# The seam of two layers: values' weights in other tiles, and the last dense products and the first values' products in one written order

## The chip, the core and the metric

The kernel runs on one core of a Trainium2 chip. The metric is the device time of one execution in microseconds. Before the change it was 1354.75 us, the median of three runs (1354.53 to 1355.81). The kernel's engines are TensorE (products, in the profile PE), VectorE (DVE), ScalarE (ACT) and GpSimd (POOL); its fetches and stores are issued by the SP engine's queue.

## The reference

The input is one sequence of 2048 rows with 640 columns. Two kinds of layer alternate, twice each, all with the same weights:

```python
x = x + _A_ref(_layernorm(x), A_wqkv, A_w_phi, A_wo)   # linear attention
x = x + _B_ref(_layernorm(x), B_w1, B_b1, B_w2)        # dense, Mish, dense
x = x + _A_ref(_layernorm(x), A_wqkv, A_w_phi, A_wo)
x = x + _B_ref(_layernorm(x), B_w1, B_b1, B_w2)
```

The attention has 32 heads of 20 columns. Queries and keys go through a small matrix per head (`w_phi`), and their features are two softmaxes, of the result and of its negative, side by side. The features of the keys times the values are summed over all rows; each query then takes the product of its features with this sum, divided by that with the sum of the features. A product with `wo` follows. The dense part is `h = x @ w1 + b1` with 1536 columns, `h * tanh(softplus(h))`, and a product with `w2`. All of it is float32.

## The kernel before

**Precision.** Each float32 operand is held as a high and a low part, and a product is made of three passes of TensorE: high by high, high by low, low by high. "Splitting" writes the two parts: ScalarE copies the high one (`split`, line 143), VectorE or GpSimd subtracts it for the low one (line 144).

**Blocks.** The 2048 rows are eight blocks (`NB`) of 256; a block is two halves of 128 rows. A layer (`LAYERS` = 2) has three stages: `attend_first` (keys, values and queries of all blocks, and the sum over the keys), `attend_second` (the queries' average and the product with `wo`) and `dense` (both dense products). `dense` walks over 8 blocks by 6 pairs of hidden column blocks: `hidden` makes 60 products (line 941) and the activation (`mish`, lines 951 to 967), and `contract` two steps later (`SKEW`) makes 24 products with `w2` (line 981) into two wide PSUM tiles per block. After the last pair, `end` adds the result to the rows (line 1026), takes their statistics, stores them (line 1032), normalises them into two row tiles (line 128), transposes these in place (line 386) and spills them in eight DMAs (line 388) as columns for the next layer (`n2_d`).

**The seam.** What is looked at here is the passage from `dense` of the first layer to `attend_first` of the second, about 655 to 715 us into the span. The first block's columns are fetched (`load_turned`, line 396) and split (`Transposed.step`, lines 128 and 332) while the last dense pairs run. `load_v_weights` takes the five blocks of 128 rows of the values' weights (line 138) into raw tiles and splits them into the `r1` tiles, which the first dense weights have left; the split's ScalarE instructions are placed behind the last exponential of `mish`. Raw block k stands in a row tile (k = 0, 1), a v tile (k = 2, 3) or a big tile (k = 4); the order is 0, 1, 4, 2, 3 (`V_ORDER`). The columns' weights for keys and queries come from DRAM, where the first layer left them (`load_k_weights`, line 213, and `load_q_weights`, line 207).

In `attend_first` of the second layer, block 0 is worked off in the order values of half 0, keys of half 0, keys of half 1, values of half 1, queries of half 0, queries of half 1. Values of half i are 30 products, 15 for each half of the columns, into two narrow PSUM tiles (`values`, `project`, `project_half`, line 416); keys and queries are 30 products into one wide PSUM tile. ScalarE copies them out. While block b is worked off, the three column chunks of block b + 1 are fetched, at the first step (`fetch_normed`), and split at the fourth to sixth.

**Tiles.** The tags that matter: row tiles ("xn", 4), x tiles of two halves of 640 columns ("x", 2), v tiles ("v", 2), big tiles ("big", 5); in PSUM, wide tiles ("mm", 2) and narrow ones ("one", 4). The three column chunks of a block take three row tiles; the two normalised halves of `end` take two.

**What sets the order.** A planner orders the instructions of each engine from the traced program, by readiness and by the order of tracing. `manual_schedule` holds the written order on the engines that it names; `contract_last`, at the very end of the kernel, does that for TensorE. `issue_after` places instructions behind another on the same engine. All ScalarE instructions that go through `act` are chained in the order in which they are written; those of `split` and `mish` do not go through it. At the seam of the kernel before, nothing is held on TensorE: the planner mixes the last 24 dense products with the values' products.

The lines that the change touches in `dense` and `attend_first`:

```python
nxt, kv_ws = first
...
pv = project(xts, i, kv_ws, D, [one_tile(), one_tile()], ks=V_ORDER)
...
if pr == n_pr - 1:
    end(b)
```

Of the kernel before, what the change touches and what calls it, by code (L numbers as in the profile page):

```python
# [16 lines left out]
P = 128  # L17
S = 2048
D = 640
# [5 lines left out]
BT = 2  # L25
BLK = BT * P
NB = S // BLK
NT = S // P
G = 11
HC = D // 2  # L30
# [7 lines left out]
SKEW = 2  # L38
V_ORDER = (0, 1, 4, 2, 3)
# [12 lines left out]
def kernel(  # L52
# [13 lines left out]
    nc = tc.nc  # L66
# [11 lines left out]
    def one_tile():  # L78
        return psum.tile([P, 512], F32, tag="one", name="one", bufs=4)
# [4 lines left out]
    def x_tile():  # L84
        return work.tile([P, BT, D], F32, tag="x", name="xt", bufs=2)
# [49 lines left out]
    def staged(src, stage):  # L135

        st = stage()[:, :D]
        nc.sync.dma_start(st, src)
        return st
# [42 lines left out]

    def v_weights(ws, low=nc.vector, ahead=False):

        def fetched(k):
            return staged(wv[k * P:(k + 1) * P, :], (row_tile, row_tile, v_tile, v_tile, big_tile)[k])

        st = {}
        if ahead:
            st = {k: fetched(k) for k in V_ORDER}  # L190
            yield
        for k in V_ORDER:
            split(ws[k][0][:, D:2 * D], ws[k][1][:, D:2 * D], st[k] if ahead else fetched(k), low)
            yield
# [205 lines left out]
    def project(xts, t, ws, col, ps=None, w=HC, ks=range(KD)):  # L400

        if ps is None:
            mm = mm_tile()
            ps = [mm[:, 0], mm[:, 1], mm]
        for c in range(2):
            project_half(ps[c], xts, t, ws, col, c, ks, w=w, final=ks[-1])
        return ps
# [65 lines left out]
    def attend_first(layer, x_src, first):  # L473
# [45 lines left out]
                if b == NB - 1:  # L519
                    yield  # L520

        def values(xts, i, v):
            vv = v.rearrange("p (h d) -> p h d", d=DH + 1)
            if i < BT:
                pv = project(xts, i, kv_ws, D, [one_tile(), one_tile()], ks=V_ORDER)
                for c in range(2):
                    act(vv[:, c * H // 2:(c + 1) * H // 2, :DH],
                        pv[c][:, :HC].rearrange("p (h d) -> p h d", d=DH), AF.Copy)
            else:
                pv = project(xts, i % BT, kv_ws, D)  # L530
                act(vv[:, :, :DH].rearrange("p (c h) d -> p c h d", c=2),
                    both(pv).rearrange("p c (h d) -> p c h d", d=DH), AF.Copy)
            act(vv[:, :, DH], ident[:, :H], AF.Copy, scale=0.0, bias=1.0)
            yield

        if first is None:
            E = mybir.EngineType
            with tc.manual_schedule(engines={E.PE, E.SP, E.Activation, E.DVE, E.Pool}):
                written[0] = True
                ps = one_tile()  # L540
                for _ in range(TURNS):
                    nc.tensor.transpose(ps[:, :P], ident, ident)  # L542
                xt = x_tile()
                rows = [row_tile() for _ in range(BT)]
# [24 lines left out]
                kv_ws = [r1_pair(k) for k in range(KD)]  # L569
# [8 lines left out]
                xts = FirstRows()  # L578
# [16 lines left out]
                turned, last = one_tile(), one_tile()  # L595
# [50 lines left out]
                vs = [v_tile() for _ in range(BT)]  # L646
                xt = fetch(x_src, 1)
# [20 lines left out]
                nxt = Transposed(nxt_rows)  # L668
# [15 lines left out]
                    advance()  # L684
                    pending.append(g)
        else:
            nxt, kv_ws = first
            load_k_weights(kv_ws)
            q_ws = load_q_weights()
        for b in range(0 if layer else 1, NB):  # L690
            xts = nxt
            order = ("k0", "k1", "v0", "v1", "q0", "q1")
            if b == 0:
                order = ("v0", "k0", "k1", "v1", "q0", "q1")
            elif b == 1 and layer == 0:
                order = ("k0", "q0", "k1", "v0", "q1", "v1")
            elif b == NB - 1:
                order = ("k0", "k1", "v0", "v1", "q0")
            vs = [v_tile() for _ in range(BT)]
            for n, (kind, t) in enumerate(order):  # L700
                t = int(t)
                i = b * BT + t
                if b == 0 and n == 1:
                    kva = one_tile()
                    nc.vector.memset(kva[:, :360], 0.0)
                if b == NB - 1 and n == 3:
                    loaded = {0: load(0), 1: load(1, lambda: x_tile().rearrange("p t d -> p (t d)"))}
                if b + 1 < NB:
                    if n == 0 and b == 1 and layer == 0:
                        with tc.issue_after(ready):  # L710
                            xt = fetch_normed(b + 1)
                    elif n == 0:
                        xt = fetch_normed(b + 1)
                    elif n == 2:
                        nxt = xt if layer else normed(b + 1, xt)
                    elif n > 2:
                        nxt.step()
                g = {"k": lambda: keys(xts, i, vs[t]), "q": lambda: queries(xts, i),
                     "v": lambda: values(xts, i, vs[t])}[kind]()
                if b == NB - 1 and n == 3:  # L720
                    advance()
                    next(g)
                else:
                    next(g)
                    advance()
                pending.append(g)
            if 0 < b <= KD and layer == 0:
                spill_qk_weights(kv_ws, q_ws, b - 1)
            if b == 1:
                five = make_five(KD, lambda k: wo[k * P:(k + 1) * P, :], ordered=True)  # L730
                next(five)
                o_ws = []
            elif 2 < b:
                o_ws.append(next(five))
# [192 lines left out]
    def dense(x_src, x_dst, w1s, w2s, first, last):  # L927
# [41 lines left out]
        def contract(b, pr, ah, al):  # L969
            final = last and b == NB - 1  # L970
            if pr == 0:
                blocks[b][2] = [mm_tile() for _ in range(BT)]
                if final:
                    blocks[b].append(one_tile())
            pys = blocks[b][2]

            def product(t, j, c, n):
                f = 2 * pr + j
                l, w = ((ah, 0), (ah, 1), (al, 0))[n]
                ps = blocks[b][3] if final and t == c == 1 else pys[t][:, c]  # L980
                nc.tensor.matmul(ps[:, :HC], l[:, j, t * P:(t + 1) * P], w2s[f][w][:, c * HC:(c + 1) * HC],  # L981
                                 start=(f == 0 and n == 0), stop=(f == KF - 1 and n == 2))

            order = [(t, j, c, n) for t in range(BT) for j in range(2) for c in range(2) for n in range(3)]
            if b == NB - 1 and pr == KF // 2 - 1:
                order = [(t, j, c, n) for j in range(2) for t in range(BT) for c in range(2) for n in range(3)]
            for o in order:
                product(*o)

        def contract_last(b, acts):  # L990
            pys, apart = blocks[b][2:]
# [58 lines left out]
        for i in range(len(steps) + SKEW):  # L1050
            if i < len(steps):
                b, pr = steps[i]
                if pr == 0 and b + 1 < NB:
                    fetch_rows_of(b + 1)
                if pr == 2 and b + 1 < NB:
                    blocks[b + 1] = [fetch(x_src, b + 1), None, None]
                if pr == 3 and (b + 1 < NB or not last):
                    nxt = load_turned(n1_d[b + 1] if b + 1 < NB else n2_d[0], (v_tile, v_tile, row_tile))
                acts[i] = hidden(b, pr)
                if b == 0 and pr == n_pr - 2:  # L1060
                    with tc.issue_after(exps[0]):
                        nxt.step()
                if pr == 1 and b + 1 < NB:
                    with tc.issue_after(exps[0]):
                        normalize(b + 1, ahead, ahead)
                    spill_turned(ahead, n1_d[b + 1])
                if pr == n_pr - 1 and (b + 1 < NB or not last):
                    if b + 1 < NB:
                        blocks[b + 1][1] = nxt
                    with tc.issue_after(exps[0]):  # L1070
                        nxt.all()
            if i <= KD:
                with tc.issue_after(exps[0]):
                    w = next(last_w2)
                if i:
                    w2s[6 + i] = w
            if i == len(steps) - 1 and not last:
                with tc.issue_after(exps[0]):
                    kv_ws = load_v_weights()
            if i >= SKEW:  # L1080
                b, pr = steps[i - SKEW]
                if not last or b < NB - 1 or pr < n_pr - 2:
                    contract(b, pr, *acts.pop(i - SKEW))
                elif pr == n_pr - 1:
                    contract_last(b, {pr - 1: acts.pop(i - SKEW - 1), pr: acts.pop(i - SKEW)})
                if pr == n_pr - 1:
                    end(b)
        return nxt, kv_ws

    with tc.block(schedule_with_timeline_sim=True):  # L1090
        src, first = x, None
# [81 lines left out]
```

## Time and profile before

| | |
|---|---|
| median of three runs | 1354.75 us |
| the profiled execution | 1355.98 us |
| its span, first to last instruction | 1354.1 us |
| TensorE busy | 1348.3 us, 12890 products |
| VectorE busy | 1069.7 us |
| ScalarE busy | 584.6 us |
| GpSimd busy | 468.9 us |
| moved by DMA | 169.21 MB |

The profile is of one execution. A row of an engine's timeline gives the start and the duration in us, the engine, the line of the kernel, the operation, the tiles written and read, their shapes and how many were merged; in brackets, the idle time of the engine before and what released it. A row of the stretches gives, for a window, busy time and number of instructions of TensorE, its weight loads, VectorE, ScalarE and GpSimd, then the granted clock of TensorE (1.00 is full), the busy share of the DMA engines and GB/s. A row of the waits gives who waited for whom: total us, times, longest. Products are pipelined, so the recorded 0.31 us of one is longer than the 0.146 us from one to the next.

### The profile page before, as it was taken

Reading aid. Unit: us, or ns where it says so; the run is one execution under the profiler, and the core shown is the slowest. Engines: PE = TensorE matmul, PEld = TensorE weight load, DVE = VectorE, ACT = ScalarE, POOL = GpSimd, SP = SyncE. Lnnn points to the kernel's source line nnn. Section 1 sums busy time; section 2 is a strip of 40 time slices with the busy share of each in tenths; the row PEclk is TensorE's granted clock in tenths of the full one; section 3 lists DMA queues with packets and bytes.
Section 4 is the critical chain, followed back from the end, with each engine's and each line's share of the span. In section 5 each row is a group of like instructions: output and inputs, shape, how many; then the busy total and the mean of one; then the engine's idle time right before and its main releaser. Section 6 shows DMA issues by size and latency. Waiting matters only on the chain.

```text
span 1354.1 us, 30937 instructions
## 1 busy us (share of the span) xinstructions
PE 1348.3 (100%) x12890; PEld 1336.8 (99%) x12890; DVE 1069.7 (79%) x1810; ACT 584.6 (43%) x1039; POOL 468.9 (35%) x357
## 2 busy tenths in 40 slices
PE   9999999999999999999999999999999999999999
PEld 9999999999999999999999999999999999999998
DVE  7988888886787888778779888888768776676775
ACT  6344444222554555445444344432236444444443
POOL 3345544444322222122225556744441211111112
PEclk9999999999999999999999999999999999999999
DMA  9623336798613543334573534468964231233200
GB/s 345 176 49 73 79 60 132 195 281 275 207 28 88 118 117 85 54 97 114 147 225 69 114 71 77 81 159 241 286 242 121 79 83 27 88 98 98 66 33 21
DMA packets 350757, 169.21 MB, mean 125 GB/s; under 512 B 287241, under 2 KB 324089, under 8 KB 350617
## 3 DMA queue, kind: packets, MB, share of 16 engines
q1 hardware_dynamic: 350617, 167.23, 46.3%
q8 instruction: 101, 1.65, 0.5%
q14 instruction: 39, 0.32, 0.1%
HBM read 104.61 MB, written 62.59 MB: 123 GB/s over the span
## 4 chain that ended last, share of the span: by engine, by line
PE 99%; DMA 1%; issue 0%; ACT 0%; DVE 0%; POOL 0%; SPq 0%; POOLq 0%
PE mm L416 28%; PE one L941 25%; PE mm L981 24%; PE one L416 13%; PE mm L801 3%; PE one L326 2%; PE one L501 2%; PE mm L273 1%; DMA v<-in_wv 1%; PE one L542 0%; PE mm L999 0%; DMA r1l<-wp_d 0%; PE one L273 0%; PE one L981 0%; PE one L801 0%; PE one L999 0%
## 5 line engine op out<-in xcount | busy, mean ns | idle before, releaser
L967 POOL TENSOR_TENSOR ol<-big,ol 128x512 fp32r<-128x512 f32 (+1 forms) x98 | 130.6, 1332 | 484.7 <-ACT ol L966 400.7
L981 PE MATMUL mm<-r2h,ol 128*128 128x320 f32 x1236 | 295.5, 309 | 0.0
L941 PE MATMUL one<-xtl,r1h 128*128 128x256 f32 x960 | 268.2, 279 | 0.0
L941 PE MATMUL one<-xth,r1l 128*128 128x256 f32 x960 | 268.0, 279 | 0.0
L941 PE MATMUL one<-xth,r1h 128*128 128x256 f32 x960 | 265.9, 279 | 0.0
L981 PEld LDWEIGHTS mm<-r2h,ol 128*128 128x128 f32 x1236 | 211.9, 188 | 0.0
L981 PE MATMUL mm<-r2l,ol 128*128 128x320 f32 x618 | 190.6, 309 | 0.0
L416 PE MATMUL mm<-r1h,xth 128*128 128x304 f32 (+1 forms) x600 | 185.1, 309 | 0.0
L416 PE MATMUL mm<-r1h,xtl 128*128 128x304 f32 (+1 forms) x600 | 183.8, 307 | 0.0
L416 PE MATMUL mm<-r1l,xth 128*128 128x304 f32 (+1 forms) x600 | 183.6, 306 | 0.0
L941 PEld LDWEIGHTS one<-xtl,r1h 128*128 128x128 f32 x960 | 180.4, 188 | 0.0
L941 PEld LDWEIGHTS one<-xth,r1l 128*128 128x128 f32 x960 | 180.4, 188 | 0.0
L941 PEld LDWEIGHTS one<-xth,r1h 128*128 128x128 f32 x960 | 179.6, 188 | 0.0
L956 DVE TENSOR_SCALAR big<-big 128x512 f32<-128x512 f32 (+1 forms) x98 | 56.3, 575 | 111.4 <-ACT big L954 111.2
L465 POOL TENSOR_TENSOR big<-big,r 128x1280 f32<-128x1280 f32 x42 | 101.4, 2419 | 69.3 <-DVE r L464 44.4
L954 ACT ACTIVATE big<-one,b1s 128x256 f32<-128x256 f32 x192 | 80.8, 467 | 91.1 <-PE one L941 90.2
L958 ACT ACTIVATE big<-big,two 128x512 f32<-128x512 f32 (+1 forms) x98 | 70.1, 716 | 115.4 <-DVE big L957 115.4
L966 ACT ACTIVATE ol<-big 128x512 fp32r<-128x512 f32 (+1 forms) x98 | 60.9, 622 | 133.5 <-DVE big L965 133.4
L981 PEld LDWEIGHTS mm<-r2l,ol 128*128 128x128 f32 x618 | 116.1, 188 | 0.0
L416 PEld LDWEIGHTS mm<-r1h,xth 128*128 128x128 f32 x600 | 112.8, 188 | 0.6
L416 PEld LDWEIGHTS mm<-r1h,xtl 128*128 128x128 f32 x600 | 112.8, 188 | 0.4
L416 PEld LDWEIGHTS mm<-r1l,xth 128*128 128x128 f32 x600 | 112.8, 188 | 0.0
(186 smaller groups left out, 3147.3 us busy)
## 6 DMA issues: line engine op xcount, KB each, us to landing
big<-e_d SPq DMA_DIRECT2D x30, 640.0 KB, 6.5
x_d<-xt SPq DMA_DIRECT2D x23, 640.0 KB, 5.1
e_d<-r SPq DMA_DIRECT2D x88, 160.0 KB, 4.0
xt<-x_d SPq DMA_DIRECT2D x22, 640.0 KB, 5.6
n_d<-xn SPq DMA_DIRECT2D x176, 80.0 KB, 2.2
xt<-in_x SPq DMA_DIRECT2D x15, 640.0 KB, 4.3
xn<-x_d SPq DMA_DIRECT2D x28, 320.0 KB, 4.2
v<-n_d SPq DMA_DIRECT2D x30, 256.0 KB, 3.4
```

What stands on the lines that cost most here:

```text
L326: nc.tensor.transpose(ps[:, c, t * P:(t + 1) * P], self.rows[t][:, (c0 + c) * P:(c0 + c + 1) * P], ident)
L416: nc.tensor.matmul(ps[:, :w], a[:, sl], r, start=(k == 0 and n == 0), stop=(k == final and n == end))
L465: nc.gpsimd.tensor_tensor(eg, eg, r.unsqueeze(2).to_broadcast([P, 2 * H, DH]), op=ALU.mult)
L501: nc.tensor.matmul(kva[32 * q:32 * q + DH + 1, c:c + 2 * DH], v[:, (DH + 1) * h:(DH + 1) * (h + 1)], e[:, 2 * DH * h:2 * DH * (h + 1)], st ...
L801: nc.tensor.matmul(po[c][64 * q:64 * q + 64, GW * j:GW * j + w], phs[g][:n, s0:s0 + 64], kvb[:n, g, :w], start=True, stop=True)
L941: nc.tensor.matmul(ph[:, j, :], l, r, start=(n == 0), stop=(n == 3 * KD - 1))
L954: exps[0] = nc.scalar.activation(part(ta, 0)[:, j - js.start], ph[:, j, :], AF.Exp, bias=b1s[:, 2 * pr + j:2 * pr + j + 1]).ins
L956: nc.vector.tensor_scalar_min(e, e, E_CAP)
L958: nc.scalar.activation(r, n, AF.Ln, bias=two)
L966: nc.scalar.activation(ah[:, js], n, AF.Copy)
L967: nc.gpsimd.tensor_tensor(al[:, js], n, ah[:, js].bitcast(F32), op=ALU.subtract)
L981: nc.tensor.matmul(ps[:, :HC], l[:, j, t * P:(t + 1) * P], w2s[f][w][:, c * HC:(c + 1) * HC], start=(f == 0 and n == 0), stop=(f == KF - 1 ...
```

## The change

The raw blocks k = 2 and 3 of the values' weights go into the two halves of one x tile, and block 4 into a row tile. (In the first layer, where `ahead` is set, the homes stay as they were.)

`contract` of the last pair of the first layer's last block issues nothing any more. It returns two functions, one for each of its two hidden column blocks, and `dense` returns them together with a third that calls `end` of that block. A new function, `between_layers`, calls them in `attend_first` of the second layer, at the first step of block 0, after the fetch of block 1's chunks has been traced. It holds TensorE's order by `manual_schedule`: 30 values' products of half 0, twelve dense products, six values' products of half 1, twelve dense products, and nine more values' products; `end` is traced ahead of these nine. Among the twelve, the eight that read the activation's high part stand first. The other 15 values' products of half 1 stay where they were, in `values`.

```diff
     def v_weights(ws, low=nc.vector, ahead=False):
 
+        halves_of_x = []
+
+        def x_half():
+            if not halves_of_x:
+                xt = x_tile()
+                halves_of_x.extend(xt[:, t] for t in range(BT))
+            return halves_of_x.pop(0)
+
         def fetched(k):
-            return staged(wv[k * P:(k + 1) * P, :], (row_tile, row_tile, v_tile, v_tile, big_tile)[k])
+            home = v_tile if ahead else x_half
+            return staged(wv[k * P:(k + 1) * P, :], (row_tile, row_tile, home, home, big_tile if ahead else row_tile)[k])
...
-        def values(xts, i, v):
+        def between_layers(xts, closing):
+            ps = [one_tile(), one_tile(), one_tile()]
+
+            def products(i, seq):
+                for n, (c, k, j) in enumerate(seq):
+                    rows, w = ((xts.hs, 0), (xts.hs, 1), (xts.ls, 0))[j]
+                    nc.tensor.matmul(ps[i + c][:, :HC], rows[k][:, i // 2 * P:(i // 2 + 1) * P],
+                                     kv_ws[k][w][:, D + c * HC:D + (c + 1) * HC],
+                                     start=(k == j == 0), stop=((k, j) == last))
+
+            with tc.manual_schedule(engines={mybir.EngineType.PE}):
+                last = 4, 2
+                for c in range(2):
+                    products(0, [(c, k, j) for k in (0, 1) for j in range(3)] + [(c, 4, 0), (c, 4, 1)])
+                products(0, [(c, k, j) for c in range(2) for k in (2, 3) for j in range(2)])
+                products(0, [(c, k, 2) for k in (2, 3, 4) for c in range(2)])
+                closing[0]()
+                last = V_ORDER[-1], 2
+                rest = [(0, k, j) for k in V_ORDER for j in range(3)]
+                products(2, rest[:6])
+                closing[1]()
+                closing[2]()
+                products(2, rest[6:])
+            return ps[:2], ps[2:]
+
+        def values(xts, i, v, pv=None):
             vv = v.rearrange("p (h d) -> p h d", d=DH + 1)
             if i < BT:
-                pv = project(xts, i, kv_ws, D, [one_tile(), one_tile()], ks=V_ORDER)
+                if pv is None:
+                    pv = project(xts, i, kv_ws, D, [one_tile(), one_tile()], ks=V_ORDER)
+                elif len(pv) == 1:
+                    pv.append(one_tile())
+                    project_half(pv[1], xts, i, kv_ws, D, 1, V_ORDER, final=V_ORDER[-1])
...
-            nxt, kv_ws = first
+            nxt, kv_ws, closing = first
...
+                if b == n == 0:
+                    pvs = between_layers(xts, closing)
                 g = {"k": lambda: keys(xts, i, vs[t]), "q": lambda: queries(xts, i),
-                     "v": lambda: values(xts, i, vs[t])}[kind]()
+                     "v": lambda: values(xts, i, vs[t], pvs[t] if b == 0 else None)}[kind]()
...
-            order = [(t, j, c, n) for t in range(BT) for j in range(2) for c in range(2) for n in range(3)]
             if b == NB - 1 and pr == KF // 2 - 1:
-                order = [(t, j, c, n) for j in range(2) for t in range(BT) for c in range(2) for n in range(3)]
-            for o in order:
-                product(*o)
+                return [lambda j=j: [product(t, j, c, n) for ns in ((0, 1), (2,)) for t in range(BT)
+                                     for c in range(2) for n in ns] for j in range(2)]
+            for t in range(BT):
+                for j in range(2):
+                    for c in range(2):
+                        for n in range(3):
+                            product(t, j, c, n)
...
-                    contract(b, pr, *acts.pop(i - SKEW))
+                    closing = contract(b, pr, *acts.pop(i - SKEW))
...
-                if pr == n_pr - 1:
+                if pr == n_pr - 1 and (last or b < NB - 1):
                     end(b)
-        return nxt, kv_ws
+        return None if last else (nxt, kv_ws, closing + [lambda: end(NB - 1)])
```

## The prediction

> **What bounds the kernel.** I read the shares of the engines first, then the same by stretches, then the list of who waited for whom on TensorE, and last, round the seam of the two layers, the chain and each engine in order of time.
>
> ```profile
> span 1354.1 us, 30937 instructions
> PE 1348.3 (100%) x12890; PEld 1336.8 (99%) x12890; DVE 1069.7 (79%) x1810; ACT 584.6 (43%) x1039; POOL 468.9 (35%) x357
> ...
> 680.00:700.00 20.00, 19.62 (x135) 19.35 (x134) 13.73 (x30) 7.44 (x16) 4.46 (x5) 1.00 0.75 255
> 700.00:1020.00 320.00, 319.19 (x3731) 314.04 (x3730) 266.12 (x409) 118.07 (x206) 164.90 (x110) 1.00 0.59 151
> ...
> PE one L542 <- POOL ident masks.py:199: 1.3, 1, 1.3
> PE mm L801 <- issue: 0.8, 1, 0.8
> PE one L416 <- ACT r1h L143: 0.4, 1, 0.4
> ```
>
> TensorE is the bound: 1348.3 of 1354.1 us busy, at a granted clock of 1.00 in the stretches shown (the column after POOL). Only three of its waits are listed, and the change bears on the last, 0.4 us at the seam. The number of products does not change. So the change can win no more than that wait; what it can lose has no such limit, since any lateness of another engine that reaches TensorE adds to the time. Here is that wait:
>
> ```profile
> 684.16 6.93 DMA v<-in_wv
> ...
> 691.11 0.75 ACT r1h L143
> ...
> 682.07 1.36 ACT L143 ACTIVATE r1h<-xn 128x640 fp32r<-128x640 f32 x2
> ...
> 691.75 0.40 ACT L966 ACTIVATE ol<-big 128x256 fp32r<-128x256 f32 x1
> 692.06 0.72 ACT L143 ACTIVATE r1h<-v 128x640 fp32r<-128x640 f32 x1
> ...
> 685.64 0.60 PE L416 MATMUL one<-r1h,xth 128*128 128x320 f32 x3
> ...
> 691.90 0.71 PE L416 MATMUL one<-r1h,xth 128*128 128x320 f32 x3 [0.38 <-ACT r1h L143]
> ...
> 696.41 0.30 PE L416 MATMUL mm<-r1h,xth 128*128 128x304 f32 x1
> ...
> 704.98 2.19 PE one L416 x15
> ```
>
> The last two blocks of the values' weights (k = 2, 3) go into v tiles, whose fetch starts at 684.16 and lands 6.9 us later; ScalarE splits the first at 691.11 and the second at 692.06, and only then can TensorE go on. From 685.64 to 696.41 TensorE works off 69 products: 30 values' products of the first half block, 15 of the second half block's first columns, and the last 24 of the dense block. At 2.19 / 15 = 0.146 us each these need 10.1 us; they took 10.77. The seam therefore costs 0.7 us, the listed 0.38 and the slower restart round it.
>
> **The change part by part.** *Other homes for the weights.* The same five fetches and five splits are made; blocks 2 and 3 go to halves of an x tile, block 4 to a row tile instead of a big one. When can they start?
>
> ```profile
> L1032 SPq DMA_DIRECT2D x_d<-xt x2: 337/359/381, 656.8 to 697.0; - x2
> 671.11 0.43 SPq L138 DMA_DIRECT2D xn<-in_wv  x1
> 681.06 0.39 SPq L138 DMA_DIRECT2D big<-in_wv  x1
> ```
>
> The store of the x tile of block 6 is issued at 656.8, so blocks 2 and 3 can come in more than 20 us before use; block 4 can follow the second row tile at 671.11 instead of starting at 681.06. The bytes on the queues are the same, only their order moves; the columns' weights loaded after them are first needed at 696.41, while the last of all these fetches has landed by 692.06, when its split starts, so I cost their shift at nothing. If that cover were gone, each block that is 1 us late would cost 1 us. This step takes away the 0.7 us: **-0.7**. Bounds: 0 (the fetches stay late) to -0.7.
>
> *The written order.* TensorE now takes k = 0, 1, 4 of both column halves, then k = 2 and 3, then the low x products, then twelve dense products, six values' products, twelve dense products, and nine values' products. Nothing is added; a strict order can wait where the old one went round. The earliest risk is the low part of block 4, the eighth product, wanted at 685.64 + 7 x 0.146 = 686.66.
>
> ```profile
> 685.18 0.81 DVE L144 TENSOR_TENSOR r1l<-xn,r1h 128x640 fp32r<-128x640 f32 x1
> 685.91 0.68 DVE L332 TENSOR_TENSOR xtl<-v,xth 128x512 fp32r<-128x512 f32 x1
> 686.50 0.42 DVE L332 TENSOR_TENSOR xtl<-xn,xth 128x256 fp32r<-128x256 f32 x1
> 686.84 0.42 DVE L963 SCALAR_TENSOR_TENSOR big<-big 128x256 f32<-128x256 f32 x1
> 688.57 0.83 DVE L144 TENSOR_TENSOR r1l<-big,r1h 128x640 fp32r<-128x640 f32 x1 [1.31 <-ACT r1h L143]
> ```
>
> VectorE has no gap from 685.18 to 687.26. If the low part of block 4 follows directly on that of block 1, it ends at 685.91 + 0.83 = 686.74, 0.1 us late; behind the three instructions that now follow, it ends near 687.2 + 0.8 = 688.0, 1.3 us late. I take **+0.1**, because its high part can follow the two that end at 682.07 + 1.36 = 683.43 and be there at 684.2, and block 1's low part went ahead of the others too; the bounds are 0 and +1.3. The dense factor's second half is wanted 48 products on (30 + 12 + 6), at 692.65; it was written from 691.75 to 692.15 even behind the late splits, so it is early enough.
>
> *The end of the last dense block moves.* Before, its adds, statistics, two normalised row tiles and eight spills are traced ahead of layer 1; now they stand behind the fetch of block 1's three column chunks, which take row tiles of the same four. What moves is two adds, six statistics, three small instructions on GpSimd, two scalings, two normalisings, two transposes, a store and eight spills. On the queue of fetches it goes behind three entries of 0.5 us (1.04 for two, below) that can be issued long before it; on VectorE and GpSimd nothing of layer 1 is ready before it.
>
> ```profile
> 697.43 1.04 SPq L396 DMA_DIRECT2D xn<-n_d  x2
> 701.83 0.88 SPq L388 DMA_DIRECT2D n_d<-xn  x2
> ...
> 703.94 2.17 SPq L388 DMA_DIRECT2D n_d<-xn  x4
> ...
> 706.28 2.81 SPq L396 DMA_DIRECT2D xn<-n_d  x2
> ...
> SPq L396 <- DMA n_d<-xn: 1.9, 2, 1.4
> ```
>
> I read from this that the tiles of one tag are given out in the order in which the program first uses them: the row tile of the weights' block 1 was last read at 685.99 (685.18 + 0.81), yet the first two chunks are fetched only at 697.43, beside the normalising; the third comes at 706.28, after a spill has freed a row tile. In the new order the three chunks come first and take three of the four, long before they are used. The first normalised half gets the fourth. The second half gets none until the first has been spilled, since the chunks are read later on the same engine. ScalarE's instructions here are chained in the written order, so everything behind that normalising waits too, and first of all the copy of the first values out of PSUM.
>
> ```profile
> 700.00 1.74 ACT L128 ACTIVATE xn<-xt,stats 128x640 f32<-128x640 f32 x2 [7.21 <-DVE stats L305]
> 701.64 0.73 ACT L128 ACTIVATE v<-one 128x320 f32<-128x320 f32 x2
> 702.39 0.67 ACT L128 ACTIVATE big<-mm 128x608 f32<-128x608 f32 x1
> ...
> L128 ACT ACTIVATE v<-one x4: 415/423/437, 701.6 to 707.2; 128x320 f32<-128x320 f32 x4
> ...
> 700.96 1.66 DVE L386 STREAM_TRANSPOSE xn<-xn 128x640 f32<-128x640 f32 x2 [0.88 <-ACT xn L128]
> ...
> DMA to landing us min/median/max: 2.2/2.3/2.4
> ...
> 704.81 0.31 PE L416 MATMUL one<-r1h,xth 128*128 128x320 f32 x1
> ...
> 695.14 1.56 DVE L1026 TENSOR_TENSOR xt<-mm,xt 128x640 f32<-128x640 f32 x2 [1.16 <-PE mm L981]
> ```
>
> The price: the first half's normalising starts at 700.00, its four spills go out from 701.83 to 703.4 (the second half's follow at 703.94), and with 2.3 us to land (the spills issued from 701 to 703) the tile is free at 705.7. The second half starts then instead of 700.87, so what follows is 4.8 us later, with the signalling 5.0. The values' first copy ended at 701.64 + 0.44 = 702.08. There are four narrow PSUM tiles, and the 15 products at 704.81 need a fifth, the one that this copy empties: a cover of 2.7 us. The dense products now end 0.8 us earlier (the add at 695.14 can start near 694.35), which widens the cover by 0.1 against products that come 0.7 us earlier. So TensorE waits 5.0 - 2.8 = **+2.2** us ahead of those 15 products. It has nothing else to do there: the queries' products need a wide PSUM tile, and both hold keys, which are copied still later. The bounds: 0, if the row tiles are given out otherwise, and about 5.0, if the spills land as slowly as the slowest of the sixteen of this stretch (5.1 instead of 2.3; the row below).
>
> ```profile
> 711.40 0.68 ACT L128 ACTIVATE r<-mm 128x608 f32<-128x608 f32 x1 [1.13 <-PE mm L416]
> ...
> 696.57 8.40 PE mm L416 x60
> ...
> DMA to landing us min/median/max: 2.2/2.6/5.1
> ```
>
> Further on, ScalarE is 5.0 - 0.8 = 4.2 us later than now and the products 1.5: the first queries' copy, which ended at 712.08, falls back by 2.7 us. The 15 products end at 704.98 + 2.19 = 707.17; its wide tile is next taken 60 products on, at 8.40 us for 60, so at 715.57: a cover of 3.5. I cost that at nothing and allow 1 us in the range; without the cover each microsecond would count.
>
> *The sum*: -0.7 + 0.1 + 2.2 = +1.6 us. The profiled execution took 1355.98, 1.9 us of it around the span, and stands 1.2 us over the median of 1354.75; the difference is added to both: 1357.6 for such an execution and **1356.35** for the median.
>
> **The rivals.** *A, the seam's gain is left alone*: no row tile is missing, because the three chunks are fetched only after the normalising. For it: that is how they stand now, at 697.43. Against it: they are now written first. It gives -0.7, or 1354.05.
>
> *B, the splits of block 4 come last on VectorE as well*: +1.3 instead of +0.1, everything behind it shifts along; 1354.75 - 0.7 + 1.3 + 2.2 = 1357.55. Against it: VectorE is idle from 687.26 to 688.57 and again later, so the late weights are what set its order now.
>
> *C, slower*: the first half's spills are held on the queue of fetches. Place: the second normalising. A spill that lands in 5.1 us, or one entry ahead of it that waits for its tile, adds 2.8 or more to 2.2; the wait is then 5 us and the time 1354.75 - 0.7 + 5.0 = 1359.05. It decides once the wait passes 3.4 us (0.7 + 2.7). If the array came back from such a gap at half its speed, the 15 products behind it would take another 2.2 us, which makes 1361.2; the rows show a clock of 1.00 with no wait over 1.3 us, so they cannot tell. [...] For it: the slowest spill of the stretch; against it: its neighbours at 701 to 703 all landed within 2.4, and the chunks that fill the queue then would have been fetched long before.
>
> *D, the weights do not come earlier*: the fetches stay behind the columns' weights, the wait of 0.7 remains and the rest comes on top; 1357.0. Against it: the x tile's store is issued at 656.8, and nothing else of this stretch takes such a tile.
>
> **How the numbers follow.** A measurement of this kernel tells about 0.2% from no change, here 2.7 us. My forecast has 0.48, A 0.24, B and D together 0.12, C 0.14, and 0.02 is for something that I have not seen which makes TensorE's own work shorter. The low end is A less the scatter of the runs, 1353.8; the high end lies between B and C, 1358.6, and leaves about a tenth of C above it. Faster by over 0.2% would need 2.7 us where the seam offers 0.7: 0.02. Slower by over 0.2% is C and the upper edge of B and of the forecast: 0.17. The rest, 0.81, is within.
>
> **What the profile after would show.** The fetches of the weights all issued before 680 (first step); no TensorE wait for ScalarE's split between 685 and 696, and the keys' first product near 695.7 (second); the three chunks of block 1 fetched before 697, a gap of some 5 us between the two normalising instructions on ScalarE, and a TensorE wait of about 2 us for the values' copy, ahead of the 15 products, near 704 (third). The prediction is wrong if the two normalising instructions still stand together, or if a wait shows up on TensorE between 685 and 696 of over 1 us.

## The result and the profile after

The changed kernel took 1357.09 us, the median of 22 runs (1356.11 to 1361.39), beside 1355.80 us for the kernel before in as many runs on the same chips (1354.38 to 1357.17). The medians are 1.3 us apart. The ratio over all runs is 1.0014, with a 95% interval of 1.0008 to 1.0020: 1.9 us slower, 1.1 to 2.7. That is within 0.2%, but on the slow side and clear of the scatter. The kernel before stood 1.05 us higher in these runs than in the three that the prediction was made from (1354.75), so the forecast is held against the differences and not against the time itself.

The list of TensorE's waits in the kernel after: who waited for whom, total us, times, longest.

```profile
PE one L425 <- ACT v L128: 1.8, 1, 1.8
PE one L580 <- POOL ident masks.py:199: 1.3, 1, 1.3
PE one L282 <- DMA raw<-in_wqk_t: 0.5, 1, 0.5
```

The wait for the split of the weights is gone; in its place there is a longer one, 1.8 us instead of 0.4, for the copy of the first values (line 128 on ScalarE). The third row is at the start of the kernel and has nothing to do with the change. ScalarE and VectorE round that wait, in order of time:

```profile
681.67 1.98 ACT L143 ACTIVATE r1h<-xn 128x640 fp32r<-128x640 f32 x3
683.56 1.35 ACT L143 ACTIVATE r1h<-xt 128x640 fp32r<-128x640 f32 x2
...
698.81 0.92 ACT L128 ACTIVATE xn<-xt,stats 128x640 f32<-128x640 f32 x1 [8.36 <-DVE stats L314]
704.41 0.92 ACT L128 ACTIVATE xn<-xt,stats 128x640 f32<-128x640 f32 x1 [4.68 <-DMA n_d<-xn]
705.24 0.74 ACT L128 ACTIVATE v<-one 128x320 f32<-128x320 f32 x2
...
684.36 1.55 DVE L144 TENSOR_TENSOR r1l<-xn,r1h 128x640 fp32r<-128x640 f32 x2
685.83 1.56 DVE L144 TENSOR_TENSOR r1l<-xt,r1h 128x640 fp32r<-128x640 f32 x2
```

All five blocks of weights are split before 687.4. The two normalising instructions, which stood together before, are 5.6 us apart, and the bracket of the second names what it waited for: a spill of the first half. The chunks that took the row tiles are in the queue's order of time:

```profile
673.22 0.66 SPq L138 DMA_DIRECT2D xn<-in_wv  x1
...
684.98 1.99 SPq L405 DMA_DIRECT2D xn<-n_d  x3
...
700.64 7.58 SPq L397 DMA_DIRECT2D n_d<-xn  x8
```

The last raw block is issued at 673.22, the three chunks of block 1 at 684.98, some 14 us ahead of the first normalising. Now TensorE at both ends of the wait, and the granted clock behind it (the column after GpSimd's busy time):

```profile
695.36 0.30 PE L425 MATMUL mm<-r1h,xth 128*128 128x304 f32 x1
...
703.62 0.30 PE L425 MATMUL mm<-r1h,xtl 128*128 128x304 f32 x1
705.70 0.41 PE L425 MATMUL one<-r1h,xth 128*128 128x320 f32 x1 [1.78 <-ACT v L128]
...
705.70:707.00 1.30, 1.30 (x9) 1.30 (x10) 0.66 (x2) 1.30 (x5) 0.00 (x0) 1.00 0.00 0
707.00:708.00 1.00, 1.00 (x6) 1.00 (x6) 1.00 (x2) 1.00 (x4) 0.00 (x0) 0.62 0.79 127
708.00:710.00 2.00, 2.00 (x10) 2.00 (x9) 2.00 (x4) 0.91 (x3) 1.28 (x1) 0.50 0.66 105
710.00:711.00 1.00, 1.00 (x7) 1.00 (x6) 1.00 (x2) 0.00 (x0) 0.00 (x0) 0.68 0.00 0
711.00:713.00 2.00, 2.00 (x16) 2.00 (x15) 1.78 (x3) 0.86 (x1) 0.00 (x0) 1.00 0.50 156
```

The 15 products start 1.94 us after the step that the stream before them would have kept. And then the clock falls: to 0.50, from about 707.2 to 710.6. That is 3.4 us at half speed (0.38 + 1.0 + 0.32 us lost of the clock in the three rows, doubled), in which a product takes 0.27 us instead of 0.146.

**A measure that is free of the scatter.** Two waits, which no part of the change touches, come and go from one execution to the next: the one for the first fetch of raw weights (0 to 1.1 us in the profiles of this study) and one in `attend_second` (listed as "issue") for nothing that the profile shows (0 to 1.3 us). Together they move the time of an execution more than the seam's 0.7 us. So beside the times I use a stretch of TensorE's chain that has neither in it: from the start of the last pair's 30 hidden products, just ahead of the seam, to the fourth sum over keys of the second layer. What happens behind its end it does not hold. In the chain of the kernel before its two ends are

```profile
675.26 3.51 PE one L941 x30
...
802.36 1.41 PE one L501 x126
```

and in that of the kernel after

```profile
674.86 3.50 PE one L981 x30
...
804.60 1.40 PE one L510 x126
```

so 127.10 and 129.74 us: the changed kernel loses 2.64 us there.

### The profile page after: what moved, and what is told of

Read it like the earlier page. It is cut to its first block, busy times and chain, and to the rows that moved or that the text cites. A ratio compares the mean times of both kernels' runs of the same rounds, so it can differ in the third digit from the quotient of the medians.

```text
span 1355.6 us, 30939 instructions
## 1 busy us (share of the span) xinstructions
PE 1348.6 (99%) x12890; PEld 1337.2 (99%) x12890; DVE 1067.7 (79%) x1810; ACT 584.6 (43%) x1039; POOL 470.9 (35%) x357
## 4 chain that ended last, share of the span: by engine, by line
PE 98%; DMA 0%; DVE 0%; SPq 0%; ACT 0%; POOL 0%; issue 0%; POOLq 0%; ACTq 0%
PE mm L425 28%; PE one L981 25%; PE mm L1021 24%; PE one L425 13%; PE mm L841 3%; PE one L335 2%; PE one L510 2%; PE mm L282 1%; PE mm L1042 0%; PE one L537 0%; PE one L282 0%; DMA raw<-in_wqk_t 0%; PE one L1021 0%; PE one L841 0%; DMA n_d<-xn 0%; ACT xn L128 0%
```

## The experiments

The table holds every run: the stretch (end less start in the chain of that run's profile), its difference from the kernel before, TensorE's wait ahead of the 15 products, whether the granted clock falls to 0.50 there, and the ratio of the times to the kernel before with its interval.

| run | stretch | difference | wait | clock falls | ratio |
|---|---|---|---|---|---|
| before | 802.36 - 675.26 = 127.10 | 0 | 0 | no | 1 |
| after | 804.60 - 674.86 = 129.74 | +2.64 | 1.78 | yes | 1.0014 (1.0008 to 1.0020) |
| e1, end before the fetch | 802.08 - 675.60 = 126.48 | -0.62 | 0 | no | 1.0002 (0.9993 to 1.0010) |
| e5, end in big tiles | 801.47 - 674.99 = 126.48 | -0.62 | 0 | no | 0.9996 (0.9987 to 1.0005) |
| e2, homes alone | 802.50 - 674.98 = 127.52 | +0.42 | 0 | no | 1.0003 (0.9994 to 1.0012) |
| e3, end behind the fetch alone | 803.64 - 675.14 = 128.50 | +1.40 | 1.46 | no | 1.0015 (1.0006 to 1.0024) |
| e4, old homes | 810.92 - 675.11 = 135.81 | +8.71 | 1.80 | yes, twice | 1.0072 (1.0059 to 1.0086) |
| e6, wait filled with 18 | 804.26 - 676.10 = 128.16 | +1.06 | 0 | no | 1.0014 (1.0005 to 1.0023) |
| e7, wait filled with 9 | 803.85 - 675.67 = 128.18 | +1.08 | 0.8 | no | 1.0009 (1.0001 to 1.0018) |
| e9, wait filled with 4 | 803.26 - 675.01 = 128.25 | +1.15 | 1.4 | no | 1.0006 (0.9997 to 1.0015) |
| e8, after again | 805.14 - 675.43 = 129.71 | +2.61 | 1.76 | yes | 1.0013 (1.0004 to 1.0023) |
| e10, a longer wait | 807.07 - 675.13 = 131.94 | +4.84 | 3.65 | yes | 1.0040 (1.0026 to 1.0054) |

**e1: the end of the dense block is traced ahead of the fetch.**

```diff
+                if b == n == 0:
+                    pvs = between_layers(xts, closing)
                 if b + 1 < NB:
...
-                if b == n == 0:
-                    pvs = between_layers(xts, closing)
```

> The changed kernel, but the last dense block's end (its adds, normalising and spills, with the whole written order) is traced ahead of the fetch of block 1's three chunks instead of behind it, so the two normalised halves get their row tiles before the chunks do. If the row tiles are the cause (theory): the two normalising instructions stand together again, TensorE does not wait ahead of the 15 values' products (1.78 us in the changed kernel), its clock stays at 1.00 behind them, and only the seam's gain is left: 0.5 to 0.9 us faster than the kernel before, some 2 to 2.5 us faster than the changed one. Rival (the written order itself delays the values' copy): the wait stays near 1.8 us and the time 1 to 2 us over the kernel before.

The two normalising instructions stand together, and TensorE has no wait between 684 and 712 us. ScalarE in order of time, and TensorE's stretches:

```profile
699.54 1.74 ACT L128 ACTIVATE xn<-xt,stats 128x640 f32<-128x640 f32 x2 [8.36 <-DMA raw<-in_wo]
701.18 0.74 ACT L128 ACTIVATE v<-one 128x320 f32<-128x320 f32 x2
...
684.00:703.00 19.00, 19.00 (x134) 19.00 (x133) 12.20 (x26) 7.13 (x16) 4.50 (x5) 1.00 0.70 231
703.00:715.00 12.00, 12.00 (x87) 12.00 (x86) 11.13 (x14) 6.30 (x12) 5.87 (x4) 1.00 0.54 114
```

The stretch is 0.62 us shorter than before. The expected 0.5 to 0.9 us in the times did not show: the medians are level (1355.62 and 1355.66). The times cannot show so little: the ratio's interval reaches from 0.9993 to 1.0010, and this run's profile happened to have both of the unrelated waits:

```profile
PE mm L841 <- issue: 1.3, 1, 1.3
PE one L282 <- DMA raw<-in_wqk_t: 1.0, 1, 1.0
```

So the place of the end behind the fetch was the cause of the new wait; TensorE's written order was not, since it is unchanged here.

**e5: the end's two halves in other tiles.** The order of the changed kernel, but tiles of another tag.

```diff
-                xn = [row_tile() for _ in range(BT)]
+                xn = [big_tile()[:, :D] if b == NB - 1 else row_tile() for _ in range(BT)]
```

> The changed kernel, but the two normalised halves of that one end stand in big tiles instead of row tiles; the order of everything else as in the changed kernel. Theory: with tiles at hand the second normalising follows the first at once and the time is that of the run with the end ahead of the fetch: 0.5 to 0.9 us faster than the kernel before. Rival (it is the order of the traced work and not the tile that holds the second half): the gap of some 4.7 us between the two stays, and the time is that of the changed kernel.

```profile
698.93 1.74 ACT L128 ACTIVATE big<-xt,stats 128x640 f32<-128x640 f32 x2 [8.36 <-DVE stats L314]
700.57 0.74 ACT L128 ACTIVATE v<-one 128x320 f32<-128x320 f32 x2
```

No gap, and the same stretch as e1 to the hundredth. Between two runs that remove the wait in different ways, by order and by tile, this leaves the shortage of row tiles as its cause. At 1355.01 us e5 has the lowest median of the experiments, and its stretch is shorter than that of both kernels; against the kernel before (1355.66 beside it) the times do not separate it (0.9996, 0.9987 to 1.0005).

**e2: the new homes alone**, in the kernel before.

```diff
-            return staged(wv[k * P:(k + 1) * P, :], (row_tile, row_tile, v_tile, v_tile, big_tile)[k])
+            home = v_tile if ahead else x_half
+            return staged(wv[k * P:(k + 1) * P, :], (row_tile, row_tile, home, home, big_tile if ahead else row_tile)[k])
```

> The kernel before with only the first part of the change: the raw blocks 2 and 3 of the values' weights in an x tile and block 4 in a row tile; no written order, the end of the dense block where it was. Theory: the late fetch was the whole cause of the seam's wait, so the homes alone win it: no wait of TensorE for the split between 685 and 696 us, 0.5 to 0.9 us faster than the kernel before. Rival (the written order is needed for the gain): a wait of 0.3 us or more stays at the seam and the time is within 0.3 us of the kernel before.

The theory failed. The split is no longer waited for, but the planner puts the dense products later among the values': the last twelve now stand directly ahead of the keys' first product (694.20 to 696.0), where six values' products stood between in the kernel before. Two other waits come up:

```profile
689.84 0.56 PE L990 MATMUL mm<-r2h,ol 128*128 128x320 f32 x2 [0.21 <-POOL ol L976]
696.45 0.41 PE L425 MATMUL mm<-r1h,xth 128*128 128x304 f32 x1 [0.33 <-DVE xt L1035]
```

0.21 us for the activation's low part, and 0.33 us because the keys' wide tile is not yet emptied by the last adds. Together 0.54 us in place of 0.38. The seam's gain needs both: the weights early and the written order, which puts nine values' products between the dense products and the keys.

**e3: the move alone**, in the kernel before: the end is traced behind the fetch, with old homes and no written order.

```diff
-                if pr == n_pr - 1:
+                if pr == n_pr - 1 and (last or b < NB - 1):
                     end(b)
...
+                if layer and b == n == 0:
+                    closing()
                 g = {"k": lambda: keys(xts, i, vs[t]), "q": lambda: queries(xts, i),
```

> The kernel before with only the move: the end of the first layer's last dense block is traced behind the fetch of block 1's three chunks; old homes, no written order. Theory: the second normalised half waits for the spills of the first, a gap of 4.5 to 5 us on ScalarE, TensorE waits some 1.5 to 2.2 us for the values' copy, and its clock drops to half behind that wait for about 3.4 us, which costs some 1.5 us more: 2.5 to 4 us slower than the kernel before. Rival (the gap on ScalarE is only harmful together with the earlier fetches or the written order): under 1 us slower.

```profile
691.75 0.71 PE L416 MATMUL one<-r1h,xth 128*128 128x320 f32 x3 [0.35 <-ACT r1h L143]
706.27 0.41 PE L416 MATMUL one<-r1h,xth 128*128 128x320 f32 x1 [1.46 <-ACT v L128]
```

The old wait at the seam is still there and the new one comes on top; the stretch is 1.40 us longer. The move alone makes the wait. The drop of the clock, which I had expected, is not in this profile, and so the stretch falls short of the expected 2.5 to 4 us. The median of the times was 2.3 us over that of the kernel before. Part of the difference lies behind the stretch: near the end of the span, at 1348.43, this profile has one more wait that the kernel before has not,

```profile
PE mm L1001 <- POOL ol L969: 0.4, 1, 0.4
```

for the low part of an activation in the last dense block. Only e4 has one like it; why it comes up in these two is open.

**e4: the old homes under the written order.**

```diff
-            home = v_tile if ahead else x_half
-            return staged(wv[k * P:(k + 1) * P, :], (row_tile, row_tile, home, home, big_tile if ahead else row_tile)[k])
+            return staged(wv[k * P:(k + 1) * P, :], (row_tile, row_tile, v_tile, v_tile, big_tile)[k])
```

> The changed kernel with the old homes of the raw weights (blocks 2 and 3 in v tiles, block 4 in a big tile), so the written order meets the late fetches. Theory: the strict order cannot go round them; block 4's low part is ready near 689.4 (fetch at 681, split at 687.8, low part at 688.57) but wanted at 686.7, so TensorE waits 2 to 3 us there, and again 2 to 3 us for blocks 2 and 3: 3 to 6 us slower than the changed kernel. Rival (the order is harmless in itself): no more than 1 us over the changed kernel.

```profile
688.24 0.41 PE L528 MATMUL one<-r1h,xth 128*128 128x320 f32 x1 [1.71 <-ACT r1h L143]
689.10 0.63 PE L528 MATMUL one<-r1l,xth 128*128 128x320 f32 x1 [0.45 <-DVE r1l L144]
692.40 0.43 PE L528 MATMUL one<-r1l,xth 128*128 128x320 f32 x1 [0.23 <-DVE r1l L144]
693.39 0.41 PE L528 MATMUL one<-r1h,xth 128*128 128x320 f32 x1 [0.56 <-ACT r1h L143]
694.25 0.42 PE L528 MATMUL one<-r1l,xth 128*128 128x320 f32 x1 [0.45 <-DVE r1l L144]
712.06 0.41 PE L416 MATMUL one<-r1h,xth 128*128 128x320 f32 x1 [1.80 <-ACT v L128]
```

A strict order stops at the first late operand: five waits of 3.4 us in all at the seam where the planner's order has 0.38, and a drop of the clock behind the first as well as behind the last. Of the two groups of waits, 2.2 us for block 4 are as expected, and 1.2 us for blocks 2 and 3 are less. The stretch is 6.1 us longer than in the changed kernel and the median 7.0 us over that of e8 beside it, just over the expected 3 to 6; the waits are 3.4 us of it and the additional drop of the clock some 1.5; about 1 us of the stretch I have not found.

**e8: the changed kernel once more**, unaltered, beside the runs with the filled wait.

> The changed kernel as it is, beside the two with the filled wait. Theory: some executions keep the clock and some lose it, so its times scatter over 3 us or more, while those with the filled wait keep within about 1 us; the profile shows the wait of 1.8 us and, if the clock fell in that execution, 0.5 between 706 and 712 us. Rival: its scatter is that of the kernel before.

The wait of 1.76 us and the drop of the clock are there again, and the stretch agrees with the first profile to 0.03 us. In these rows the stretches are of TensorE alone (busy time, number, granted clock, DMA's share, GB/s):

```profile
PE one L425 <- ACT v L128: 1.8, 1, 1.8
...
706.00:708.00 2.00, 1.76 (x8) 0.67 0.15 25
708.00:710.00 2.00, 2.00 (x9) 0.50 0.88 142
710.00:712.00 2.00, 2.00 (x16) 0.98 0.02 2
```

The scatter of the times says little: 3.7 us here, 3.2 in the kernel before beside it. But the mean granted clock of every execution is on record, to a thousandth, and one drop takes 1.7 us of 1356, or 0.00125. In e8 four executions have a mean of 1.000 and took 1356.0 to 1357.5 us; six have 0.999 or 0.998 and took 1358.5 to 1359.7. Of the 22 runs of the result, 13 have 1.000 (median 1356.67) and nine have less (median 1358.89). So some 15 of 32 executions of the changed kernel lost the clock, the two that were profiled among them, and by the medians these were 2.2 to 2.4 us slower. The mean takes in what comes behind the last product too: in e1's profile the last product ends at 1351.1 and every stretch of 2 us up to 1352 has 1.00, but the one from 1343 to 1366 has 0.93; so the clock falls when no product is left, and that alone makes its 0.999. This is rare: of 151 executions of the kernel before and of e1, e2, e3, e5, e6, e7 and e9, six are at 0.999 and none is lower.

**e6, e7, e9: the wait filled** with 18, 9 or 4 products that nobody reads, in unused columns of a wide tile; they are work beyond the reference's.

```diff
+            if layer and i == 1:
+                for _ in range(18):
+                    nc.tensor.matmul(ps[1][:, 320:512], xts.hs[0][:, :P], kv_ws[0][0][:, :192], start=True, stop=True)
             yield from features(ps, e, False)
```

> The changed kernel with 18 products whose results nobody reads (192 columns, into the unused columns of the wide tile of keys of half 1), issued right ahead of the 15 values' products, where TensorE waits. They take some 1.5 to 2 us, so they fill the wait; the values' copy is late as before. Theory (the wait costs itself and then a drop of the clock): no idle of over 0.6 us there, the granted clock stays at 1.00 between 706 and 712 us, and the time is 1 to 2 us under the changed kernel, some 0.5 to 1.5 us over the kernel before. Rival (the clock drops for another reason than the idle time): the clock is at 0.5 for some 3.4 us all the same, and the time is that of the changed kernel.

> As the run before, with 9 such products, so that about half of the wait of 1.9 us stays: 0.8 to 1.1 us idle. If the clock drops by the length of the idle time with a threshold between 1 and 1.8 us: clock 1.00, time as with 18. If any idle of about 1 us can bring it down: 0.5 for some 3.4 us, time as the changed kernel.

> The changed kernel with 4 products whose results nobody reads ahead of the 15 values' products, so that some 1.3 to 1.5 us of the wait of 1.8 stay. Runs so far: clock down to 0.5 in the two profiles with 1.8 us idle, 1.00 in the ones with 1.5, 1.3 and 0.8. Theory (a limit between 1.5 and 1.8 us): the clock holds, the stretch from the last pair's hidden products to the fourth sum over keys is 1.1 us longer than in the kernel before, and the times keep within 2.5 us. Rival (a matter of chance at any idle time of this size): the clock falls in the profile or the times reach over 3 us above their lowest.

```profile
704.99 2.15 PE L508 MATMUL mm<-r1h,xth 128*128 128x192 f32 x18
706.98 0.36 PE L425 MATMUL one<-r1h,xth 128*128 128x320 f32 x1
```

With 18 the wait is full: the values' products follow the last of them without a gap. The clock stays at 1.00 in all three profiles, and in 32 of their 33 executions the mean is 1.000. The three stretches agree: 1.06, 1.08 and 1.15 us over the kernel before, whether 0, 0.8 or 1.4 us of the wait stay idle. So the late copy costs 1.7 us by itself (0.62 + 1.1), filled or not, and the drop of the clock another 1.5 (2.64 - 1.1). The expectation of the times of e6, 1 to 2 us under the changed kernel, was met against e8 (1357.52 to 1358.54) and not against the first 22 runs (1357.09); the stretch settles what the times leave open. That the times would keep within about 1 us was not met: they spread over 1.9 to 2.3 us. Four useless products remove the drop; e9's stretch of TensorE behind its wait of 1.4 us:

```profile
706.00:708.00 2.00, 2.00 (x14) 1.00 0.31 50
```

**e10: the wait doubled**: the second normalising is done three times, with the same result.

```diff
                 normalize(b, xn, [xt[:, t, :] for t in range(BT)])
+                if b == NB - 1:
+                    for _ in range(2):
+                        act(xn[1], xt[:, 1, :], AF.Identity, bias=stats[:, b, 1, 1:2], scale=stats[:, b, 0, 1:2])
```

> The changed kernel with the second normalising done three times instead of once (the same result twice more), which keeps ScalarE busy 1.75 us longer ahead of the values' copy, so that TensorE waits some 3.5 us. Theory (the drop of the clock is one more price of fixed size once the wait is long enough): the clock is at 0.5 for some 3.4 us behind the wait in the profile, and the stretch named above is 4.3 to 4.6 us longer than in the kernel before (2.6 and 1.75); the times no longer fall into two groups, since every execution loses the clock: 3 to 5 us over the kernel before. Rival (the drop grows with the wait): it lasts 5 us or more and the stretch is over 5.5 us longer.

```profile
704.64 2.83 ACT L128 ACTIVATE xn<-xt,stats 128x640 f32<-128x640 f32 x3 [4.65 <-DMA n_d<-xn]
...
707.84 0.41 PE L425 MATMUL one<-r1h,xth 128*128 128x320 f32 x1 [3.65 <-ACT v L128]
```

The wait grows by 1.9 us and the stretch by 2.2 (4.84 against 2.64); the clock is low for the same 3.4 us. In this execution the drop has the size that it had behind the shorter wait; the remaining 0.3 us I have not found, and the stretch is a little over the expected 4.3 to 4.6. All five executions have a mean clock below 1.000, so every one of them seems to lose it, as expected. But three of them, the slowest (1361.5 to 1363.0), have 0.997: at least 3.4 us of the clock are missing there (0.0025 x 1361), twice what one drop takes (the slowest of the 22 runs of the changed kernel, 1361.39, has 0.997 too), and the median is 5.4 us over the kernel before instead of the expected 3 to 5. So a fixed price is shown for the profiled execution alone (1360.09 us; its mean of 0.998 is a little more than the one drop of 0.00125 makes, and since every other stretch of 2 us up to 1352 has 1.00, the rest is lost behind 1352, in the last 6 us of its span of 1358.0). Whether the low clock lasted longer in the other three, as the rival has it, is open; they have no profile.

## Why the prediction came out as it did

The forecast was +1.6 us, 1356.35 us, with a range of 1353.8 to 1358.6. The measured 1357.09 us lies in it, and the ratio makes the loss 1.9 us. By its steps:

- **The bound and the price of the seam** (-0.7) were right in size: e1 and e5, which have this and nothing else, are 0.62 us shorter, and the keys' first product starts 10.12 us after the first values' product (685.24 to 695.36) instead of 10.77. (That the change can win no more than the listed wait of 0.4 us, as the reading of the bound has it, was too low; the priced 0.7 was right.) The step that gave it to the new homes alone was wrong: e2 shows that the planner's order then loses 0.54 us elsewhere. It needs the written order too.
- **The written order** (+0.1, up to 1.3) costs nothing here. Block 4's low part followed directly on block 1's (the pair at 684.36 on VectorE), as I had taken it. The danger that I bounded at 1.3 us is real, and e4 shows it where the weights are late.
- **The end of the dense block** (+2.2) was right in place, cause and mechanism: the second normalising 4.7 us later than in line (5.6 apart instead of 0.87; forecast 4.8), released by a spill, the wait ahead of the 15 products, the three chunks long in their tiles. It measured 1.94 us from product to product, and 1.7 in the stretch: the spills landed within 2.17 us, and the four went out a little faster. The 0.2 us for the signalling, which no row of the prediction and no run gives, is 0.1 here, from the landing at 704.30 to the start at 704.41.
- **The clock** is the step that failed. I let it stay whole for a wait of 2.2 us, and kept its drop for a wait of 5 us, in rival C. It fell behind 1.8 us, for 3.4 us, and that is 1.5 of the 2.64 us lost in the two profiled executions; by the mean clock it fell in 15 of 32.
- **The sum** is -0.6 instead of -0.7, +0 instead of +0.1, +1.7 instead of +2.2, and +1.5 in those executions that lose the clock, instead of nothing: +1.1 without the drop and +2.6 with it, where the forecast has +1.6. The medians of the two groups of the 22 runs stand 0.9 and 3.1 us over the kernel before (1356.67 and 1358.89 beside 1355.80). That the forecast came so near the 1.9 us of the ratio is in part luck: a wait that was priced too high stood in for a drop that was priced at nothing. The path of the wait was no luck.
- **The rivals.** A did not happen; it is what e1 and e5 make. B and D did not happen either. Of C the slower array was right, and it came at C's place; the late spills and the wait of some 5 us, which it was made to hang on, did not happen and were not needed.

## What to carry to other kernels

Where tiles of one tag are given out in program order, moving a step behind a fetch that takes the same tiles can starve it, even though the fetch is early and harmless in itself; count the tiles in the new order, and look for what is chained behind the starved instruction. A written order and early operands go together: each alone won nothing here, and the order with late operands lost 6 us more. Where unrelated waits move the time of an execution by 1 us, compare a stretch of the chain between two fixed products beside the times, and look for new waits outside it. And where the clock of TensorE falls behind a wait, as it did here behind 1.71 us and more, a few products that nobody reads can cost less than the wait left empty: with four of them, which left 1.4 us of it, the stretch was 1.5 us shorter.

## What the runs showed of the hardware

The granted clock of TensorE fell to 0.50 behind waits of 1.71, 1.76, 1.78, 1.80 and 3.65 us, and stayed at 1.00 behind one of 1.46, and of 1.4 and 0.8 us; in all five it stayed down for about 3.4 us. (The 1.71 us are the first wait of e4, where another of 0.45 follows 0.4 us later.) It did not fall when the wait ended, but 0.4 to 1.5 us later. The stretches of 2 us in which the two drops of e4 begin, of TensorE alone (busy time, number, granted clock, DMA's share, GB/s):

```profile
688.00:690.00 2.00, 1.31 (x4) 0.76 1.04 380
...
712.00:714.00 2.00, 1.94 (x10) 0.74 0.24 38
```

At 0.50 after the drop, a mean of 0.76 puts its beginning at 689.04 and one of 0.74 the other at 712.96: 0.80 and 0.90 us behind the ends of the waits, at 688.24 and 712.06. In e10 the stretch from 708 to 710 has 0.69, which puts the beginning at 708.76, 0.92 us behind the end of the wait at 707.84.

What decides whether the clock falls is not shown. In these profiles the shortest wait with a drop behind it is 1.71 us and the longest without one is 1.46. But by the mean clock only some 15 of 32 executions of the changed kernel lost it, and those that kept it have no profile; so how long they waited is open.
